# Four buffers for converted weight halves in a one-core attention-and-MLP kernel, with six relay buffers placed behind the mixing and the lead's score copies on ScalarE

## The chip, the cores and the metric

One core of a Trainium2 chip. The metric is the device time of one execution in microseconds (us). The engines are TensorE (PE, with its weight loads as PEld), VectorE (DVE), ScalarE (ACT), GpSimd (POOL) and SyncE (SP, which here only issues DMAs). The inputs are in HBM; wide scratch tensors in HBM (`x2`, `wsc`) are written and read back by the kernel itself.

## The reference, cut to what matters

```python
# q, k, v: (4, 12, 448, 64); w_pre, w_post: (12, 12); w_in: (768, 2048); w_out: (2048, 768); alpha: (2048,)
scores = np.matmul(q, k.transpose(0, 1, 3, 2)) / np.sqrt(64)
scores = np.einsum('bhij,hg->bgij', scores, w_pre)          # mix heads before the softmax
scores = scores - np.max(scores, axis=-1, keepdims=True)
attn = np.exp(scores)
attn = attn / (np.sum(attn, axis=-1, keepdims=True) + 1e-09)
attn = np.einsum('bhij,hg->bgij', attn, w_post)             # mix heads after the softmax
x = np.matmul(attn, v).transpose(0, 2, 1, 3).reshape(4 * 448, 768)
h = x @ w_in
g = np.maximum(h, 0.0) + alpha * np.minimum(h, 0.0)
out = g @ w_out
```

The two weight matrices arrive as 64-bit floats, so the kernel gets their raw 64-bit words and rounds them to 32-bit floats itself.

## The kernel before

The program has two streams of work that are interleaved by hand in one order (`manual_schedule`: each engine and each DMA queue executes its instructions in the order in which the code writes them). The loop `step(n)` runs for n from -1 to 94; most of the order is set there.

**Attention.** The queries of a batch are cut into chunks of 60 (or 30) rows. `qk` makes a chunk's raw scores in three parts (p = 0, 1, 2), each copied from PSUM into a score tile `st` (two buffers, tag `s`). `relay` moves rows of `st` by DMA on SP's queue into a mixing layout: groups of 10 query rows by 12 heads in `sr` tiles, which come from a ring of `NSR` constant buffers. Step n mixes groups 2n and 2n+1: `mix(n)` multiplies two `sr` tiles by `wk` on PE and VectorE takes the row maximum (`nm`, line 207); `exp(n)` follows on ScalarE (line 214), `norm(n-1)` on VectorE (lines 221 to 225), `post(n-2)` on PE (line 238) with a copy into `at` on ScalarE (line 244). When a set of chunks is complete, `pv` multiplies by v (line 261) and its two halves are added by ScalarE and VectorE into `xe` (lines 267, 268), which goes to `x2`. There are 90 mixing steps. PSUM is four double banks `p`, handed out in the order in which they were freed.

**Conversion.** `convert` goes through 64 half units (16 feature blocks, w_in and w_out, two halves of 384 columns). For each, GpSimd's queue fetches the raw words `cr` (four buffers), and `round_f64` runs five VectorE steps (lines 60, 64, 65, 66, 67) with two GpSimd operations between (lines 61, 62). Line 64 is the first to write `ct`, line 67 the last; then SP's queue stores `ct` to `wsc` (line 299). `ce` and `ct` have two buffers each. The order of the five steps of neighbouring units is woven: (i,0), (i,1), (i-1,3), (i-1,4), (i,2). In the lead (steps up to 26) a step of the program holds seven of these VectorE steps, later eight until the 64 units are done.

**MLP ("moe").** After the lead the four token blocks go through both weight matrices. `load_w` brings the converted weights `wr` back on GpSimd's queue, `split_w` splits each into a rounded part (ScalarE, line 340) and a remainder (GpSimd, line 341), and PE multiplies (lines 394 and 427). `split_x` does the same for the tokens on VectorE (lines 449, 450). `PACE` says how much of this work stands in each step.

**SP's queue.** At the start of `step(n)`, ahead of `mix(n)`, `relays(2 * (n + RA + 1))` orders the relays of two groups, which step n+3 will mix. A relay into an `sr` buffer waits until the mixing that read the buffer last is over. At the end of a step, `flush()` orders what was put into `later`: the stores of `ct`, of `xe` and of the output.

Of the kernel before, what the change touches and what calls it, by code (L numbers as in the profile page):

```python
# [8 lines left out]
F32 = mybir.dt.float32  # L9
F32R = mybir.dt.float32r  # L10
I32 = mybir.dt.int32
# [8 lines left out]
B, H, S, D = 4, 12, 448, 64  # L20
DM, DFF = 768, 2048
NT = B * S
HI = 5
HP = HI * H
# [8 lines left out]
NJ = S // 64  # L33
SR0 = 4
RA = 3
NSR = 2 * (RA + 1)
WARM = 12
LAG = 2
TB = [(b * S, S) for b in range(B)]
# [6 lines left out]
CU = DM // 2  # L46
# [24 lines left out]
def talking_heads_prelu(ctx: ExitStack, tc: tile.TileContext, q, k, v, w_pre, w_post, mask, w_in, w_out, alpha, out):  # L71
    nc = tc.nc
# [49 lines left out]
    alpha_sb = cst.tile([128, NFC], F32, name="alpha_sb")  # L122
    wk = cst.tile([128, 64], F32, name="wk")
    wq = cst.tile([128, H, HI], F32, name="wq")
    mask_sb = cst.tile([128, 2, HI, H], F32, name="mask_sb")
    wb = cst.tile([128, 2, H], F32, name="wb")
    sr_b = [cst.tile([128, S], F32, name=f"sr{i}") for i in range(NSR)]
    q_b = [cst.tile([128, 8 + NP * CW], F32, name=f"q{i}") for i in range(3)]
    a_t = cst.tile([128, NS, H, AW], F32, name="at")
# [5 lines left out]
    later = []  # L135
# [34 lines left out]
    def qk(ci, p, copy=nc.scalar.copy):  # L170
        b, c = chunks[ci]
        pt = grab()
        cn = CHUNKS[c][1]
        for cc in range(2):
            for r in range(2):
                h = slice(64 * r, 64 * r + 64)
                nc.tensor.matmul(pt[64 * cc:64 * cc + 64, r, :S], q_t[ci][h, (3 * cc + p) * cn + SR0 * cc:(3 * cc + p) * cn + SR0 * cc + 64],  # L177
                                 k_t[b, p][h, cc, :], start=True, stop=True)
        if p == 0:
            s_t[ci] = sp.tile([128, 2, 3, S], F32, tag="s", name=f"st{ci}")  # L180
        copy(s_t[ci][:, :, p, :], pt[:, :, :S])  # L181
        free(pt)
        done_qk.add((ci, p))
# [16 lines left out]
    def mix(n):  # L200
        to = m_t[n] = grab()
        ga, gb = sr_t.pop(2 * n), sr_t.pop(2 * n + 1)
        for hf, g in ((0, ga), (64, gb)):
            for u, r in ((0, slice(0, 64)), (1, slice(64, SR0 + GP))):
                nc.tensor.matmul(to[hf:hf + 64, u, :S], wk[r, :], g[r, :], start=True, stop=True)  # L205
        nm = sm.tile([128, 2], F32, tag="nm", name=f"nm{n}")
        nc.vector.tensor_reduce(out=nm, in_=to[:, :, :S], axis=AX.X, op=ALU.max, negate=True)  # L207
        nm_t[n] = nm
# [64 lines left out]
            in_=xe[:, :3 * cn].rearrange("p (c i) -> p c i", c=3)[:, :, skip:]))  # L273


    def flush():
        now, later[:] = list(later), []
        for f in now:
            f()

    def convert():
        todo = [(f, x, c) for f in range(NFC) for x in range(2) for c in range(0, DM, CU)]
        raw_c = {}

        def fetch_c(i):
            if i < len(todo):
                f, x, c = todo[i]
                raw_c[i] = cvp.tile([128, CU], I64, tag="cr", bufs=4, name=f"cr{f}_{x}_{c}")
                nc.gpsimd.dma_start(out=raw_c[i], in_=(w_in, w_out)[x][f, :, c:c + CU])

        def unit(i):
            f, x, c = todo[i]
            raw = raw_c.pop(i)
            e = cvp.tile([128, CU], I32, tag="ce", name=f"ce{f}_{x}_{c}")
            t = cvp.tile([128, CU], I32, tag="ct", name=f"ct{f}_{x}_{c}")
            for j, op in enumerate(round_f64(nc, raw, e, t)):
                op()
                if j == 4:
                    later.append(lambda: (stored.add((f, x, c)), nc.sync.dma_start(out=wsc[f, :, x * DM + c:x * DM + c + CU], in_=t.bitcast(F32))))
                    fetch_c(i + 4)  # L300
                yield

        for i in range(4):
            fetch_c(i)
        yield
        n = len(todo)
        seq = []
        for i in range(n + 1):
            seq += [(i, 0), (i, 1)] if i < n else []
            seq += [(i - 1, 3), (i - 1, 4)] if i else []  # L310
            seq += [(i, 2)] if i < n else []
        units = {}
        for i, j in seq:
            if j == 0:
                units[i] = unit(i)
            next(units[i], None)
            yield
# [156 lines left out]
    with tc.manual_schedule():  # L474
# [8 lines left out]
        nc.vector.memset(warm.bitcast(F32), 0.0)  # L483
        for _ in range(WARM):
            nc.tensor.matmul(pairs[3][:, 0, :S], warm[:, :128], warm, start=True, stop=True)
        nc.gpsimd.memset(mask_sb, 0.0)
        nc.gpsimd.memset(wb, 0.0)
        own = mask[:HP, :HI, :].rearrange("(i h) j g -> i h j g", h=H)
        wide = lambda w, n: w.rearrange("(o h) g -> o h g", o=1).to_broadcast([HI, n, H])
        for u in range(2):  # L490
# [30 lines left out]
        def relays(upto, dmas):  # L521
            nonlocal relayed
            while relayed < min(upto, NG) and (groups[relayed][0], NP // 2 - 1) in done_qk:
                relay(relayed, dmas)
                relayed += 1

        relays(4, (nc.sync, nc.scalar))
        relays(2 * (RA + 1), (nc.sync,))
        next(conv)
        for ci in (2, 3):  # L530
            load_q(ci)
# [28 lines left out]
        def step(n):  # L560
            step_now[0] = n
            if n == 1:
                for hx in range(2):
                    load_v(0, hx)
            if n >= 0:
                relays(2 * (n + RA + 1), (nc.sync,))
            due = pv_at.get(n)
            lead = n <= ready[0]
            pace = 0.0 if lead else PACE[min(cur, 2)]
            if live(n):  # L570
                mix(n)
            if live(n - 1):
                norm(n - 1)
            if due is not None:
                b = pvs[due][0]
                for hx in range(2):
                    pv(due, hx)
                    if due + 1 < len(pvs) and pvs[due + 1][0] != b:
                        load_v(b + 1, hx)
            if live(n - LAG):  # L580
                post(n - LAG)
            if live(n):
                exp(n)
            for ci, p in qk_at.get(n, []):
                b = chunks[ci][0]
                qk(ci, p, nc.vector.tensor_copy if lead and p == 1 else nc.scalar.copy)
                if ci + 1 < NC and chunks[ci + 1][0] != b:
                    load_k(b + 1, p)
                if p == 2 and ci + 3 < NC:
                    load_q(ci + 3)  # L590
            if lead:
                converts(CONV_LEAD)
            else:
                moe_work(n, pace * 0.5)
                converts(CONV_T0 // 2)
                moe_work(n, pace * 0.5)
                converts(CONV_T0 // 2)
            flush()
            for t in range(len(TB)):
                if n == ready[t] - 1:  # L600
                    load_x(t, 0)
                    load_x(t, 1)
                if n == ready[t] and t == 0:
                    for _ in split_x(0):
                        pass
                    nxt_x[0] = iter(())
            if n == ready[0] - 3:
                for u in range(2):
                    for x in range(2):
                        load_w(u, x)  # L610
                for u in range(2):
                    split_w(u, 0)
                    load_w(u + 2, 0)
# [43 lines left out]
```

## Time and profile before

| | us |
|---|---|
| median of 3 runs | 1092.49 (1086.48 to 1092.76) |
| the profiled execution's own time | 1092.34 |
| its span, first to last instruction | 1090.5 |
| PE busy | 894.5 (82%) |
| VectorE busy | 604.7 (55%) |
| ScalarE busy | 421.5 (39%) |
| GpSimd busy | 480.0 (44%) |

The busy shares are averages over stages that have different limits, so they don't say what bounds any of them. The profiled execution's own time is 1.84 us more than its span and within 0.2 us of the median, so a sum made against the profile can be carried to the median unchanged.

### The profile page before, as it was taken

Reading aid. Unit: us, or ns where it says so; the run is one execution under the profiler, and the core shown is the slowest. Engines: PE = TensorE matmul, PEld = TensorE weight load, DVE = VectorE, ACT = ScalarE, POOL = GpSimd, SP = SyncE. Lnnn points to the kernel's source line nnn. Section 1 sums busy time; section 2 is a strip of 40 time slices with the busy share of each in tenths; the row PEclk is TensorE's granted clock in tenths of the full one; section 3 lists DMA queues with packets and bytes.
Section 4 is the critical chain, followed back from the end, with each engine's and each line's share of the span. In section 5 each row is a group of like instructions: output and inputs, shape, how many; then the busy total and the mean of one; then the engine's idle time right before and its main releaser. Section 6 shows DMA issues by size and latency. Waiting matters only on the chain.

```text
span 1090.5 us, 28930 instructions
## 1 busy us (share of the span) xinstructions
PE 894.5 (82%) x12204; PEld 701.7 (64%) x12204; DVE 604.7 (55%) x1090; ACT 421.5 (39%) x769; POOL 480.0 (44%) x563
## 2 busy tenths in 40 slices
PE   5555564555777977879799999997999999899997
PEld 2234352345455656657578787786787888779996
DVE  4565664556596685774456444544645464354443
ACT  1333332322243433345445555643545454222220
POOL 6432333334364465543424553443235343447661
PEclk7767686685798988999999999999999999899999
DMA  7655566567466476544654454445544342444322
GB/s 184 201 157 175 161 168 158 163 175 229 133 187 191 142 196 189 168 136 126 184 171 131 135 157 125 134 124 161 178 123 138 120 119 73 121 124 126 102 78 76
DMA packets 79730, 161.82 MB, mean 148 GB/s; under 512 B 26276, under 2 KB 64304, under 8 KB 79600
## 3 DMA queue, kind: packets, MB, share of 16 engines
q0 software_dynamic: 21312, 90.58, 31.2%
q1 hardware_dynamic: 57432, 68.18, 18.7%
q8 instruction: 96, 1.57, 0.6%
q10 hardware_dynamic: 856, 1.21, 0.5%
q14 instruction: 34, 0.28, 0.1%
HBM read 97.62 MB, written 23.59 MB: 111 GB/s over the span
## 4 chain that ended last, share of the span: by engine, by line
PE 53%; DMA 22%; DVE 14%; issue 4%; POOL 2%; SPq 2%; ACT 1%; ACTq 0%; POOLq 0%; DVEq 0%
PE p L427 18%; PE p L394 17%; DMA wsc<-ct 17%; PE p L261 5%; PE p L238 5%; PE p L205 4%; PE p L177 4%; DVE ce L66 3%; DVE ct L67 3%; DMA sr<-st 2%; DVE ct L64 2%; POOL ws L341 2%; DVE nm L207 2%; SPq L198 1%; DMA xr<-x 1%
## 5 line engine op out<-in xcount | busy, mean ns | idle before, releaser
L341 POOL TENSOR_TENSOR ws<-wr,ws 128x768 fp32r<-128x768 f32 x128 | 235.9, 1843 | 277.9 <-ACT ws L340 276.2
L427 PE MATMUL p<-g,ws 128*128 128x448 f32 x1152 | 259.6, 380 | 23.5 <-POOL ws L341 13.1
L394 PE MATMUL p<-xs,ws 128*128 128x448 f32 x1152 | 258.9, 379 | 10.2 <-DVE xs L449 8.0
L427 PEld LDWEIGHTS p<-g,ws 128*128 128x128 f32 x1152 | 222.0, 195 | 63.0 <-POOL ws L341 17.0
L394 PEld LDWEIGHTS p<-xs,ws 128*128 128x128 f32 x1152 | 218.1, 193 | 53.9 <-issue 18.6
L214 ACT ACTIVATE e<-p,nm 128x448 f32<-128x448 f32 x180 | 112.5, 632 | 195.7 <-DVE nm L207 133.6
L238 PEld LDWEIGHTS p<-r,e 64*64 64x64 f32 x5040 | 113.7, 149 | 113.0 <-issue 68.9
L238 PE MATMUL p<-r,e 64*64 64x60 f32 x5040 | 119.5, 239 | 71.8 <-DVE r L225 34.0
L244 ACT COPY at<-p 128x960 f32<-128x960 f32 x88 | 86.3, 981 | 177.7 <-PE p L238 176.8
L340 ACT CAST ws<-wr 128x768 fp32r<-128x768 f32 x128 | 103.9, 844 | 117.8 <-issue 51.9
L207 DVE TENSOR_REDUCE nm<-p 128x2 f32<-128x896 f32 x90 | 97.7, 1086 | 90.2 <-PE p L205 90.0
L363 DVE TENSOR_TENSOR acc<-p,acc 128x896 f32<-128x896 f32 x84 | 91.3, 1087 | 87.5 <-PE p L427 87.4
L177 PE MATMUL p<-k,q 64*64 64x448 f32 x768 | 115.7, 655 | 23.0 <-DVE xe L268 8.4
L205 PE MATMUL p<-sr,wk 64*64 64x448 f32 (+1 forms) x720 | 102.5, 608 | 38.0 <-ACT at L249 12.4
L261 PEld LDWEIGHTS p<-at,v 64*64 64x64 f32 x3360 | 97.2, 150 | 34.6 <-ACT e L214 19.6
L261 PE MATMUL p<-at,v 64*64 64x120 f32 (+2 forms) x3360 | 99.5, 268 | 23.0 <-ACT e L214 17.1
L64 DVE TENSOR_SCALAR ct<-cr 128x384 int32<-128x384 int32 x64 | 29.7, 464 | 132.7 <-DMA wsc<-ct 132.7
L348 DVE TENSOR_SCALAR t<-p,alpha_sb 128x448 f32<-128x448 f32 x64 | 43.4, 678 | 93.9 <-PE p L394 93.9
L332 POOL DMA_DIRECT2D wr<-wsc x128 | 71.8, 561 | 39.4 <-POOL ws L341 34.7
L181 ACT COPY st<-p 128x896 f32<-128x896 f32 x84 | 74.9, 911 | 12.9 <-PE p L177 6.5
L205 PEld LDWEIGHTS p<-sr,wk 64*64 64x64 f32 (+1 forms) x720 | 28.6, 147 | 75.1 <-issue 40.5
L61 POOL TENSOR_SCALAR ce<-ce 128x384 int32<-128x384 int32 x64 | 33.4, 521 | 78.0 <-DVE ce L60 76.4
(48 smaller groups left out, 655.3 us busy)
## 6 DMA issues: line engine op xcount, KB each, us to landing
wr<-wsc POOLq DMA_DIRECT2D x128, 384.0 KB, 3.7
sr<-st SPq DMA_DIRECT2D x332, 105.0 KB
cr<-in_w_in_dram POOLq DMA_DIRECT2D x32, 384.0 KB, 4.0
cr<-in_w_out_dram POOLq DMA_DIRECT2D x32, 384.0 KB, 4.0
wsc<-ct SPq DMA_DIRECT2D x64, 192.0 KB
xr<-x SPq DMA_DIRECT2D x24, 224.0 KB
out_dram<-acc SPq DMA_DIRECT2D x12, 448.0 KB
q<-in_q_dram POOLq DMA_DIRECT2D x54, 90.0 KB, 4.3
```

The costliest lines, as they stand in the source:

```text
L177: nc.tensor.matmul(pt[64 * cc:64 * cc + 64, r, :S], q_t[ci][h, (3 * cc + p) * cn + SR0 * cc:(3 * cc + p) * cn + SR0 * cc + 64], k_t[b, p][ ...
L205: nc.tensor.matmul(to[hf:hf + 64, u, :S], wk[r, :], g[r, :], start=True, stop=True)
L207: nc.vector.tensor_reduce(out=nm, in_=to[:, :, :S], axis=AX.X, op=ALU.max, negate=True)
L214: nc.scalar.activation(out=e_t[n][:, u], in_=m_t[n][:, u, :S], func=AF.Exp, bias=nm_t[n][:, u:u + 1], scale=1.0, accum_out=se_t[n][:, u:u ...
L238: nc.tensor.matmul(dst[:, :, HI * u:HI * u + HI], e[h, u, 64 * jb:64 * jb + 64], r[h, u].rearrange("p (h i) -> p h i", h=H), start=True, s ...
L244: nc.scalar.copy(at[:, :, col:col + 2 * GI].rearrange("p q (g i) -> p g q i", g=2), pt[:, :, :NS * GP].rearrange("p g (q i) -> p g q i", i ...
L261: nc.tensor.matmul(to[64 * t:64 * t + 64, r, cl * cn:(cl + 1) * cn], v_t[b, hx][pr, s, (2 * cl + t) * D:(2 * cl + t + 1) * D], a_t[pr, s, ...
L340: nc.scalar.copy(t[:, 0], w)
L341: nc.gpsimd.tensor_tensor(t[:, 1], w, t[:, 0], ALU.subtract)
L363: nc.vector.tensor_tensor(dst, pt[:, :, :N], dst, ALU.add)
L394: nc.tensor.matmul(pt[:, f % 2, :S], w[:, tw, c * 128:(c + 1) * 128], xs[:, tx, c, :], start=(j == 0), stop=(j == 3 * NCC - 1))
L427: nc.tensor.matmul(pt[:, d, :S], w[:, tw, (c + d) * 128:(c + d + 1) * 128], g[:, tg], start=(j == 0), stop=(j == 3 * FG - 1))
```

## The change

Four edits. The `ct` tiles of the conversion get four buffers in place of two, and their stores go into a list `ripe` with the number of the step, which is emptied at the start of the next step (or at once when more than two wait, or when `load_w` asks). The relays of a step stand behind `mix(n)` in place of ahead of it, and the `sr` ring has six buffers in place of eight. In the lead the copies of the scores for p = 1, which VectorE made, go to ScalarE like the others. The constants `mask_sb` and `wb` lose tiles of their own and live in a buffer of the `xr` tag, which is first needed much later.

```diff
-NSR = 2 * (RA + 1)
+NSR = 2 * RA
...
-    mask_sb = cst.tile([128, 2, HI, H], F32, name="mask_sb")
-    wb = cst.tile([128, 2, H], F32, name="wb")
+    setup = xrp.tile([128, S], F32, tag="xr", name="setup")
+    mask_sb = setup[:, :2 * HP].rearrange("p (u j g) -> p u j g", u=2, g=H)
+    wb = setup[:, 2 * HP:2 * HP + 2 * H].rearrange("p (u g) -> p u g", u=2)
...
-    def flush():
+    ripe = []
+
+    def flush(upto=None):
+        while ripe and (upto is None or ripe[0][0] <= upto or len(ripe) > 2):
+            ripe.pop(0)[1]()
         now, later[:] = list(later), []
...
-            t = cvp.tile([128, CU], I32, tag="ct", name=f"ct{f}_{x}_{c}")
+            t = cvp.tile([128, CU], I32, tag="ct", bufs=4, name=f"ct{f}_{x}_{c}")
...
-                    later.append(lambda: (stored.add((f, x, c)), nc.sync.dma_start(out=wsc[f, :, x * DM + c:x * DM + c + CU], in_=t.bitcast(F32))))
+                    ripe.append((step_now[0], lambda: (stored.add((f, x, c)), nc.sync.dma_start(
+                        out=wsc[f, :, x * DM + c:x * DM + c + CU], in_=t.bitcast(F32)))))
...
-        relays(2 * (RA + 1), (nc.sync,))
+        relays(2 * RA, (nc.sync,))
...
-            if n >= 0:
-                relays(2 * (n + RA + 1), (nc.sync,))
             due = pv_at.get(n)
             lead = n <= ready[0]
             pace = 0.0 if lead else PACE[min(cur, 2)]
+            flush(n - 1)
             if live(n):
                 mix(n)
+            if n >= 0:
+                relays(2 * (n + RA + 1), (nc.sync,))
...
-                qk(ci, p, nc.vector.tensor_copy if lead and p == 1 else nc.scalar.copy)
+                qk(ci, p)
...
-            flush()
+            flush(n - 1)
```

**SP's queue in the lead.** The number behind a tile's name is that of its allocation; `wsc<-ct` is a store, `sr<-st` a relay of one group (two DMAs). Before, from the store of the fourth half unit on:

```order
L299 DMA wsc<-ct_1_384_298 128x384
L299 DMA wsc<-ct_0_0_343 128x384
L195 DMA sr_122<-st_283 60x1x448 x2
L195 DMA sr_123<-st_283 60x1x448 x2
L299 DMA wsc<-ct_0_384_418 128x384
L195 DMA sr_124<-st_283 60x1x448 x2
L195 DMA sr_125<-st_283 60x1x448 x2
L299 DMA wsc<-ct_1_0_485 128x384
```

The same place now:

```order
L304 DMA wsc<-ct_1_384_292 128x384
L304 DMA wsc<-ct_0_0_337 128x384
L196 DMA sr_117<-st_277 60x1x448 x2
L196 DMA sr_118<-st_277 60x1x448 x2
L304 DMA wsc<-ct_0_384_412 128x384
L196 DMA sr_119<-st_277 60x1x448 x2
L196 DMA sr_120<-st_277 60x1x448 x2
L304 DMA wsc<-ct_1_0_479 128x384
```

The sequence of stores and relays is the same, because nothing else stands on SP's queue between the end of one step and the start of the next; what changed is the ring behind the `sr` names (six numbers in place of eight), so that a relay of step n fills the buffers that `mix(n)` has just read, where it filled those of `mix(n-1)`.

**SP's queue at the end of the lead**, where the tokens `xr` of the first block are loaded from `x2`. Before:

```order
L271 DMA x_57<-xe_0_2643 128x3x28
L271 DMA x_57<-xe_1_2688 128x3x28
L299 DMA wsc<-ct_0_384_2566 128x384
L439 DMA xr_2_2752<-x_57 128x448
L439 DMA xr_3_2756<-x_57 128x448
L439 DMA xr_4_2760<-x_57 128x448
L439 DMA xr_5_2764<-x_57 128x448
L195 DMA sr_122<-st_2396 60x1x448 x2
```

Now:

```order
L272 DMA x_57<-xe_0_2637 128x3x28
L272 DMA x_57<-xe_1_2682 128x3x28
L445 DMA xr_2_2745<-x_57 128x448
L445 DMA xr_3_2749<-x_57 128x448
L445 DMA xr_4_2753<-x_57 128x448
L445 DMA xr_5_2757<-x_57 128x448
L304 DMA wsc<-ct_0_384_2560 128x384
L196 DMA sr_117<-st_2390 60x1x448 x2
```

One store has moved behind four token loads; one step earlier another has moved behind two. These are the only two places of the whole program at which SP's sequence of stores, relays and loads differs.

**VectorE in a step of the lead.** `nm`, `s` and `r` are the row maximum and the normalization, `ct` and `ce` the conversion. Before:

```order
L207 TENSOR_REDUCE nm_651<-p_132 128x2
L221 TENSOR_SCALAR s_653<-se_617 128x2
L222 RECIPROCAL s_653<-s_653 128x2
L225 TENSOR_TENSOR r_656<-wq,s_653 128x120
L181 COPY st_695<-p_131 128x2x448
L64 TENSOR_SCALAR ct_1_0_640<-cr_1_0_557 128x384
L66 SCALAR_TENSOR_TENSOR ce_0_384_628<-cr_0_384_492,ce_0_384_628 128x384
```

Now:

```order
L208 TENSOR_REDUCE nm_641<-p_129 128x2
L222 TENSOR_SCALAR s_647<-se_611 128x2
L223 RECIPROCAL s_647<-s_647 128x2
L226 TENSOR_TENSOR r_650<-wq,s_647 128x120
L64 TENSOR_SCALAR ct_1_0_634<-cr_1_0_551 128x384
L66 SCALAR_TENSOR_TENSOR ce_0_384_622<-cr_0_384_486,ce_0_384_622 128x384
```

The score copy is gone from VectorE here, and at ten more places; apart from these eleven and two memsets for the missing `sr` buffers, VectorE's order is the same. The eleven copies stand on ScalarE now, between the exponentials of a step and the copy `at` of the next.

## Rows read from the trace of the kernel before

**Rows 1.** The chain that ended last: shares of the span by engine, then by line

```profile
PE 53%; DMA 22%; DVE 14%; issue 4%; POOL 2%; SPq 2%; ACT 1%; ACTq 0%; POOLq 0%; DVEq 0%
PE p L427 18%; PE p L394 17%; DMA wsc<-ct 17%; PE p L261 5%; PE p L238 5%; PE p L205 4%; PE p L177 4%; DVE ce L66 3%; DVE ct L67 3%; DMA sr<-st 2%; DVE ct L64 2%; POOL ws L341 2%; DVE nm L207 2%; SPq L198 1%; DMA xr<-x 1%
```

**Rows 2.** Stretches: length, busy by engine (instructions), PE clock, DMA share, GB/s

```profile
26.80:263.10 236.30, 130.42 (x2636) 88.89 (x2628) 137.86 (x305) 78.99 (x161) 86.20 (x150) 0.73 0.60 176
263.10:291.80 28.70, 18.95 (x320) 13.76 (x320) 10.71 (x26) 4.45 (x9) 4.45 (x8) 0.64 0.59 171
291.80:474.10 182.30, 144.45 (x1786) 108.70 (x1786) 136.58 (x235) 70.69 (x128) 101.92 (x129) 0.90 0.59 170
508.50:936.00 427.50, 411.77 (x6254) 330.42 (x6246) 215.58 (x368) 209.19 (x383) 182.92 (x170) 0.99 0.47 136
```

**Rows 3.** VectorE's waits, 26.8 to 263.1 us: total us, times, longest

```profile
DVE ct L64 <- DMA wsc<-ct: 92.4, 35, 8.6
DVE nm L207 <- PE p L205: 5.2, 1, 5.2
```

**Rows 4.** VectorE's waits, 291.8 to 474.1 us

```profile
DVE ct L64 <- DMA wsc<-ct: 34.7, 16, 6.4
DVE t L348 <- PE p L394: 6.7, 2, 3.4
```

**Rows 5.** Timeline, 101 to 108 us, VectorE and SP's queue: start, length, idle before

```profile
101.49 0.56 DVE L67 TENSOR_TENSOR ct<-ct,ce 128x384 f32<-128x384 f32 x1
...
101.97 0.55 DVE L65 SCALAR_TENSOR_TENSOR ct<-cr,ct 128x384 f32<-128x384 uint32 x1
102.08 0.33 SPq L299 DMA_DIRECT2D wsc<-ct  x1
...
102.51 3.39 SPq L195 DMA_DIRECT2D sr<-st  x4
...
106.10 0.36 DVE L64 TENSOR_SCALAR ct<-cr 128x384 int32<-128x384 int32 x1 [3.31 <-DMA wsc<-ct]
106.38 1.08 DVE L207 TENSOR_REDUCE nm<-p 128x2 f32<-128x896 f32 x1
```

**Rows 6.** Groups by line and shape, 26.8 to 263.1 us: busy us, mean ns

```profile
L207 DVE TENSOR_REDUCE nm<-p 128x2 f32<-128x896 f32 x27 | 29.3, 1084 | 5.2 <-PE p L205 5.2
...
L62 POOL TENSOR_SCALAR ce<-ce 128x384 int32<-128x384 int32 x36 | 18.9, 525 | 3.0
L61 POOL TENSOR_SCALAR ce<-ce 128x384 int32<-128x384 int32 x36 | 18.1, 503 | 47.1 <-DVE ce L60 46.7
L181 ACT COPY st<-p 128x896 f32<-128x896 f32 x20 | 18.1, 904 | 3.6 <-PE p L177 1.4 <-PE p L205 1.1 <-DMA sr<-st 1.1
...
L181 DVE COPY st<-p 128x896 f32<-128x896 f32 x11 | 12.0, 1092 | 2.5 <-DMA sr<-st 1.8 <-PE p L177 0.3
```

**Rows 7.** DMA issues, 26.8 to 263.1 us: KB each, us to landing

```profile
cr<-in_w_in_dram POOLq DMA_DIRECT2D x18, 384.0 KB, 4.0
...
v<-in_v_dram POOLq DMA_DIRECT2D x4, 576.0 KB, 9.1
```

**Rows 8.** Waits of the whole span, ScalarE for weights that come back

```profile
ACT ws L340 <- DMA wr<-wsc: 12.0, 2, 10.2
```

**Rows 9.** Timeline, 250 to 259 us: one pv on PE, and a collision of VectorE and GpSimd

```profile
250.93 1.82 POOL L341 TENSOR_TENSOR ws<-wr,ws 128x768 fp32r<-128x768 f32 x1
250.98 2.19 DVE L65 SCALAR_TENSOR_TENSOR ct<-cr,ct 128x384 f32<-128x384 uint32 x1
...
253.38 5.16 PE L261 MATMUL p<-at,v 64*64 64x30 f32 x165
```

**Rows 10.** A stretch in which the DMA engines were full (columns as in rows 2)

```profile
160.00:170.00 10.00, 7.46 (x274) 6.57 (x268) 4.35 (x11) 4.02 (x9) 5.04 (x9) 0.78 1.01 242
```

**Rows 11.** Waits of the whole span, TensorE for relayed rows

```profile
PE p L205 <- DMA sr<-st: 7.1, 2, 6.1
```

**Rows 12.** Waits of SP's queue over the whole span, for the mixing

```profile
SPq L195 <- PE p L205: 79.6, 39, 7.0
```

More of the change, by code (lines that the diff above doesn't have):

```diff
@@ L485, in talking_heads_prelu @@
             nc.tensor.matmul(pairs[3][:, 0, :S], warm[:, :128], warm, start=True, stop=True)
-        nc.gpsimd.memset(mask_sb, 0.0)
-        nc.gpsimd.memset(wb, 0.0)
+        nc.gpsimd.memset(setup[:, :2 * HP + 2 * H], 0.0)
         own = mask[:HP, :HI, :].rearrange("(i h) j g -> i h j g", h=H)
```

## The prediction

> **What bounds the kernel now.** I first read the chain that ended last [rows 1]. TensorE has half of it, most of that in the last 580 us: from 508.5 to 936 us it is busy 411.8 of 427.5 us at a clock of 0.99 [rows 2], and nothing in this change takes work from it. The entry to look at is the 17% of the DMA `wsc<-ct`. A store can only be on the chain if somebody waits for it to land. So I cut the span at the starts of the row maxima of steps 0, 26, 27 and 44 and read each stretch for itself [rows 2]: A, 26.8 to 263.1 us (26 steps of the lead); B, 263.1 to 291.8 (the step in which the first tokens are loaded and split); C, 291.8 to 474.1 (the MLP has begun, the conversion still runs).
>
> In A no engine is full: TensorE 130.4, VectorE 137.9, ScalarE 79.0, GpSimd 86.2 of 236.3 us, and the clock is 0.73, a mixture of the two levels 1.2 and 2.4 GHz. The waits say which engine sets the pace. VectorE waited 92.4 us in 35 pieces for stores of `ct`, and once for 5.2 us for the mixing [rows 3]; 137.9 + 92.4 + 5.2 = 235.5 of 236.3 us, so it is always at work or waiting for a store. The timeline shows one round [rows 5]: line 67 finishes a `ct` at 102.05, SP issues its store at 102.08, and line 64, which wants that buffer, starts at 106.10, after an idle 3.31 us. The row maximum of the next step stands behind line 64 on VectorE, so it starts at 106.38, and the whole attention step hangs on it. A step takes 9.1 us on average (the 27 row maxima [rows 6] begin 26 steps in 236.3 us). In C the same wait takes 34.7 us in 16 pieces [rows 4], with TensorE at 144.5 and VectorE at 136.6 of 182.3 us.
>
> **The change part by part.**
>
> *Four `ct` buffers.* With two, line 64 of unit k+2 needs the store of unit k. In the woven order only two VectorE operations lie between line 67 of k and line 64 of k+2 (line 65 of k+1, line 60 of k+2), some 1 us (0.55 us for line 65 [rows 5], the other is shorter) against the 4.05 us that the store takes in rows 5. With four, line 64 of unit k+4 needs it, and ten more operations lie between, twelve in all. A step holds seven, so this is 12/7 of a step. VectorE's own work is 137.9 - 12.0 (the moved copies, below) = 125.9 us in 26 steps, 4.8 us each, so at its fastest the distance is 12/7 x 4.8 = 8.3 us. The store must wait for SP at worst through one set of relays, 3.39 us [rows 5], and then 4 us: 7.4 us. So an ordinary store comes back in time, and the 92.4 us go. A store of the slow kind (8.6 us [rows 3]) comes back after 12.0 and costs some 3.7 us.
>
> *What is late next in A.* VectorE's work and its other waits, 125.9 + (236.3 - 137.9 - 92.4 = 6.0) = 131.9 us. TensorE's 130.4 us and the DMA engines' 0.60 x 236.3 = 141.8 us [rows 2] come close beside it, and they hardly met before because all of them waited together. I add what appears when the steps close up. Five `pv` lie in A, and VectorE's adds to `xe` stand behind them; one half of such a `pv` pair took TensorE half of 5.16 us [rows 9], which nothing covers if TensorE is no longer ahead: 5 x 2.6 = 13 us. ScalarE stood still 12.0 us for the first weights that come back [rows 8], its exponentials behind it; half of it reaches VectorE: 6 us. Three stretches of about 10 us have full DMA engines (one is rows 10); there the store above and the fetch of `cr` (4.0 us, but 9.1 us for the large loads it shares a queue with [rows 7], against a distance of eleven operations, 7.5 us) come late, 3 us each: 9 us. Together 131.9 + 13 + 6 + 9 = 160 us. The DMA engines would then be busy 141.8/160 = 0.89 of the time and TensorE 0.82, at today's clock; denser work may raise that clock, which I don't count. A gains 236.3 - 160 = 76 us. Its bounds: 142 us, the DMA engines' own time (gain 94), and the rivals below.
>
> *B.* Its chain is load of v, `pv`, store to `x2`, token loads, split; stores of `ct` have one small part in it. Now two of them stand behind token loads on SP, and behind them the relays as before. Nobody needs these stores soon, four buffers cover them. Gain between 0 and 5 us; I take 2.
>
> *C.* VectorE's work with its other waits is 182.3 - 34.7 = 147.6 us; TensorE's 144.5 us of work at the 96% that it reaches from 508.5 us on are 150.5. With two engines so near each other, and TensorE waiting for VectorE in places, I don't expect 150.5: I take 162, a little more than half of the way. Gain 20; bounds 0 and 32.
>
> *Relays behind the mixing, six buffers.* Relays of step n now wait for `mix(n)`, where they waited for `mix(n-1)`, and SP's queue waits with them: the next stores of `ct` and `xe`, token loads and output stores stand behind. A store of step n is made by VectorE after the row maximum of step n, which itself waits for `mix(n)`; so SP is held from nothing that could go earlier, but for the 3.39 us of issuing. The relays are needed by `mix(n+3)`. At 160/26 = 6.2 us a step these are 18 us, less 3.39 for issue and up to 9.1 (the slowest landing that rows 7 show) leaves 5 us. Later, at about 10 us a step, it is 15 and more. TensorE waited for relays 7.1 us in the whole span, in two pieces [rows 11], though SP's queue already waited for the mixing 39 times [rows 12]. I take nothing; bounds 0 and +6.
>
> *Eleven copies from VectorE to ScalarE.* Minus 11 x 1.09 = 12.0 us on VectorE, plus 11 x 0.90 = 9.9 us on ScalarE [rows 6], which has 79.0 of 160 us and carries 88.9 then. It is in the sum above. A new wait is possible: the copies wait for relays that still read the score buffer, and exponentials stand behind them. VectorE met this once, 1.8 us [rows 6].
>
> *The shared setup tile* is over long before its buffer is needed, and two memsets less run at a time when VectorE has nothing else: 0.
>
> **The sum.** 76 + 2 + 20 = 98 us off the profiled 1092.3 us: **994 us**, the same against the median. With each part at its best bound, 94 + 5 + 32 = 131: 961.
>
> **The rivals.**
>
> *The DMA engines bind.* In A they moved 176 GB/s x 236.3 us = 41.6 MB; when full they moved 242 GB/s [rows 10], which makes 172 us. If the 13 and 6 us of `pv` and weights don't overlap with this, A takes 191 us and gains 45; C, with later arrivals, gains 10; B 2. That is 57: **1035 us**. For it: three stretches are full today. Against it: over all of A the share is 0.60, so most bytes move without crowding. The Trainium skill ("DMA: Bandwidth & Descriptors", section Specifications) puts the limit from HBM at about 358 GB/s for one core; by that the 41.6 MB would be 116 us, an estimate from that page, and this rival would fall. No stretch of 10 us here that I show reaches it, so the measured rate stands.
>
> *VectorE and GpSimd get in each other's way more.* At 250.9 us a GpSimd subtraction and line 65 started together, and line 65 took 2.19 us [rows 9] where it takes 0.55 alone [rows 5]. Lines 61 and 62 occupy GpSimd 18.1 + 18.9 = 37 us in A [rows 6]. With VectorE idle for 92 us these had room; packed, each may hold up a VectorE operation. Half of them on top of A gives 178.5, a gain of 58; C, in which GpSimd is busy 101.9 us, gains 10; B 2: 70 in all, **1022 us**; all of them on top of A, 1041. This is a rule of the Trainium skill as well ("SBUF — State Buffer", section Who interferes with whom): a VectorE instruction with two SBUF inputs and a GpSimd instruction that reads SBUF share a port, and the second to start stands still for all of the first. The trace agrees, 2.19 against 0.55 us.
>
> *It doesn't do what it says.* The wait for the store is replaced by another of the same length on the same chain, the fetch of `cr` or SP's queue: **about 1088 us**, the copies' part left over. Against it: the distance of 8.3 us worked out above, and no wait for `cr` in rows 3.
>
> *Slower.* The relays land after `mix(n+3)` wants them, since they can't start before `mix(n)`, and TensorE waits for them from step 27 to 89, where its time is the kernel's. To be slower it has to lose more than 98 us in 63 steps, 1.6 us a step; at 1.8 us, 113 us: **1107 us**. It decides from a time of three steps, some 30 us there, between `mix(n)` and the landing. Rows 5 and 7 show 3.4 + 9.1 = 12.5.
>
> **How the numbers follow.** Chances: the forecast, between 961 and 1012 us, 0.62; DMA engines 0.13; VectorE with GpSimd 0.14; better than all bounds (a higher clock in A) 0.04; nothing moves 0.04; slower 0.03. A measurement of this kernel can tell about 1%, 11 us, from no change: the first four cases are faster, 0.93; 0.04 the same; 0.03 slower. The range from 958 to 1040 takes in the first three cases up to their ends.
>
> **What the next profile would show.** Right: VectorE's wait at line 64 for `wsc<-ct` falls from 92.4 us in A and 34.7 in C to under 25 together; the steps of the lead take about 6.2 us; step 27 begins near 214 us in place of 292; VectorE is over 70% busy in A and the DMA share over 0.8; the last 580 us keep their length. Wrong by a rival: the DMA share in A at 1.0 with stores of over 8 us; or lines 65 to 67 with means well over 0.6 us; or TensorE waiting at line 205 for `sr<-st`. The prediction falls if the steps of the lead stay at 9 us although line 64 no longer waits: then another engine's chain had the same length all along. A smaller miss would come from C, if TensorE's waits there are not VectorE's doing.

## The result, and the profile after

The changed kernel takes 1002.91 us (median of 4 runs, 998.6 to 1005.61) against 1090.8 us before (median of four runs; the 1092.49 ahead of the prediction is that of three of them): a ratio of 0.920, 95% interval 0.915 to 0.924. 994 was forecast, with 958 to 1040 as the range. The profiled execution has a span of 1002.6 us.

The chain that ended last, by engine and by line (the changed file's lines are one to six higher than before: 208 is the row maximum that was 207, 304 the store that was 299, 347 the subtraction on GpSimd that was 341):

```profile
PE 61%; DVE 13%; DMA 10%; issue 7%; POOL 4%; ACT 3%; SPq 1%; POOLq 0%; ACTq 0%; DVEq 0%
PE p L433 20%; PE p L400 19%; PE p L262 7%; DMA sr<-st 6%; PE p L239 6%; PE p L206 5%; PE p L178 4%; POOL ws L347 2%; DVE nm L208 2%; DVE ce L66 2%; DMA wsc<-ct 2%; DVE g L361 1%; DMA xr<-x 1%; DVE ct L65 1%; DVE ct L64 1%
```

The stores `wsc<-ct` had 17% of the chain [rows 1] and have 2%. The relays have taken a part of their place, 6% in place of 2.

The same stretches as in [rows 2], cut at the same row maxima (A, B, C, and the rest): length, then busy us of PE, PEld, VectorE, ScalarE and GpSimd with instructions, clock, DMA share, GB/s:

```profile
25.90:195.80 169.90, 119.28 (x2636) 76.52 (x2628) 129.17 (x294) 86.23 (x171) 93.02 (x150) 0.80 0.84 246
195.80:222.10 26.30, 17.82 (x320) 12.46 (x320) 11.20 (x26) 4.58 (x11) 4.92 (x9) 0.69 0.60 183
222.10:380.90 158.80, 137.90 (x1785) 103.85 (x1785) 142.53 (x235) 70.82 (x128) 103.82 (x129) 0.93 0.68 196
380.90:1002.60 621.70, 589.95 (x7410) 485.79 (x7408) 310.21 (x498) 263.15 (x467) 270.75 (x242) 0.98 0.44 128
```

A fell from 236.3 to 169.9 us, B from 28.7 to 26.3, C from 182.3 to 158.8; the rest, which was 1090.5 - 474.1 = 616.4, grew to 621.7, and the start is 0.9 us shorter. Together that is 66.4 + 2.4 + 23.5 - 5.3 + 0.9 = 87.9 us, the difference of the two spans. (The prediction calls the end of C step 44. Counted, it is the row maximum of step 42, and this is how I cut here. The times of the stretch are not touched by it.)

VectorE's waits in A, after [rows 3]:

```profile
DVE nm L208 <- PE p L206: 19.0, 6, 5.7
DVE nm L208 <- ACT st L182: 8.5, 1, 8.5
DVE xe L269 <- ACT xe L268: 7.7, 6, 1.9
DVE ct L64 <- DMA wsc<-ct: 5.5, 2, 4.5
DVE xe L269 <- DMA sr<-st: 2.3, 1, 2.3
```

One of the six pieces of the first line, 5.58 us, ends where A begins and so lies ahead of it; the other five are 13.4 us. The same holds for the 5.2 us of [rows 3], which the prediction counts into A. The first row maximum after, and before (start, length, idle before):

```profile
25.94 1.09 DVE L208 TENSOR_REDUCE nm<-p 128x2 f32<-128x896 f32 x1 [5.58 <-PE p L206]
26.77 1.09 DVE L207 TENSOR_REDUCE nm<-p 128x2 f32<-128x896 f32 x1 [5.19 <-PE p L205]
```

Of the 26 steps in A, 17 take 4.3 to 5.4 us, nearly all of it VectorE's work; the other nine take 6.4 to 13.3 us and hold 84.6 of the 169.9 us. The timeline of one of the short ones, which answers to [rows 5] (start, length):

```profile
82.94 0.74 DVE L67 TENSOR_TENSOR ct<-ct,ce 128x384 f32<-128x384 f32 x1
83.60 1.08 DVE L208 TENSOR_REDUCE nm<-p 128x2 f32<-128x896 f32 x1
83.70 0.33 SPq L304 DMA_DIRECT2D wsc<-ct  x1
84.12 3.38 SPq L196 DMA_DIRECT2D sr<-st  x4
...
85.93 0.36 DVE L64 TENSOR_SCALAR ct<-cr 128x384 int32<-128x384 int32 x1
...
88.50 1.08 DVE L208 TENSOR_REDUCE nm<-p 128x2 f32<-128x896 f32 x1
```

Line 67 ends at 83.68 and line 64 starts at 85.93 without any idle time ahead of it, 2.2 us after the store was issued, a way that takes 4 us in [rows 5]; the next row maximum begins 4.9 us after the last one. That is the 4.8 us of pure VectorE work on which the prediction's distance was worked out. The wait at line 64 is 5.5 us in the whole span, where it was 132.7:

```profile
L64 DVE TENSOR_SCALAR ct<-cr 128x384 int32<-128x384 int32 x64 | 29.7, 464 | 132.7 <-DMA wsc<-ct 132.7
```

### The profile page after: what moved, and what is told of

The parts are those of the page before. It is cut to its first block, busy times and chain, and to the rows that moved or that the text cites. A ratio compares the mean times of both kernels' runs of the same rounds, so it can differ in the third digit from the quotient of the medians.

```text
span 1002.6 us, 28904 instructions
## 1 busy us (share of the span) xinstructions
PE 877.3 (87%) x12204; PEld 685.0 (68%) x12204; DVE 602.6 (60%) x1077; ACT 428.8 (43%) x780; POOL 489.3 (49%) x562
## 3 DMA queue, kind: packets, MB, share of 16 engines
q0 software_dynamic: 21312, 90.58, 33.6%
## 4 chain that ended last, share of the span: by engine, by line
PE 61%; DVE 13%; DMA 10%; issue 7%; POOL 4%; ACT 3%; SPq 1%; POOLq 0%; ACTq 0%; DVEq 0%
PE p L433 20%; PE p L400 19%; PE p L262 7%; DMA sr<-st 6%; PE p L239 6%; PE p L206 5%; PE p L178 4%; POOL ws L347 2%; DVE nm L208 2%; DVE ce L66 2%; DMA wsc<-ct 2%; DVE g L361 1%; DMA xr<-x 1%; DVE ct L65 1%; DVE ct L64 1%
## 5 line engine op out<-in xcount | busy, mean ns | idle before, releaser
L400 PEld LDWEIGHTS p<-xs,ws 128*128 128x128 f32 x1152 | 216.3, 191 | 51.7 <-issue 13.4
L239 PEld LDWEIGHTS p<-r,e 64*64 64x64 f32 x5040 | 107.5, 141 | 67.4 <-issue 43.4
L239 PE MATMUL p<-r,e 64*64 64x60 f32 x5040 | 112.4, 229 | 27.7 <-issue 12.0
L178 PE MATMUL p<-k,q 64*64 64x448 f32 x768 | 107.7, 611 | 24.4 <-ACT st L182 13.1
L206 PE MATMUL p<-sr,wk 64*64 64x448 f32 (+1 forms) x720 | 106.6, 614 | 25.6 <-ACT at L250 9.3
L262 PEld LDWEIGHTS p<-at,v 64*64 64x64 f32 x3360 | 90.7, 143 | 18.9 <-issue 16.5
L262 PE MATMUL p<-at,v 64*64 64x120 f32 (+2 forms) x3360 | 91.7, 257 | 7.1 <-issue 3.6
L182 ACT COPY st<-p 128x896 f32<-128x896 f32 x95 | 84.2, 913 | 30.4 <-DMA sr<-st 20.1
L161 POOL DMA_DIRECT2D q<-in_q_dram x62 | 38.3, 626 | 79.7 <-PE p L178 79.6
L61 POOL TENSOR_SCALAR ce<-ce 128x384 int32<-128x384 int32 x64 | 36.7, 574 | 67.9 <-DVE ce L60 65.4
```

Of the source, the lines that this page charges most:

```text
L239: nc.tensor.matmul(dst[:, :, HI * u:HI * u + HI], e[h, u, 64 * jb:64 * jb + 64], r[h, u].rearrange("p (h i) -> p h i", h=H), start=True, s ...
L262: nc.tensor.matmul(to[64 * t:64 * t + 64, r, cl * cn:(cl + 1) * cn], v_t[b, hx][pr, s, (2 * cl + t) * D:(2 * cl + t + 1) * D], a_t[pr, s, ...
L400: nc.tensor.matmul(pt[:, f % 2, :S], w[:, tw, c * 128:(c + 1) * 128], xs[:, tx, c, :], start=(j == 0), stop=(j == 3 * NCC - 1))
```

## The experiments

Each experiment changes the changed kernel by a few lines, but for the ninth, which starts from the kernel before. In one view, the medians, and the lengths of A, B and C, of steps 42 to 89, and of what follows, read from the row maxima of one profiled execution each, which need not be at its kernel's median:

| kernel | median us | A | B | C | 42 to 89 | rest |
|---|---|---|---|---|---|---|
| before | 1090.8 | 236.3 | 28.7 | 182.3 | 434.8 | 181.6 |
| changed | 1002.9 | 169.8 | 26.3 | 158.8 | 439.1 | 182.6 |
| two `ct` | 1091.1 | 234.4 | 29.8 | 180.4 | 437.5 | 182.1 |
| three `ct` | 1006.4 | 175.9 | 23.4 | 159.3 | 437.6 | 181.8 |
| copies on VectorE | 1010.8 | 176.5 | 25.3 | 158.8 | 439.5 | 182.5 |
| stores as before | 1003.4 | 168.7 | 24.5 | 159.6 | 439.1 | 182.3 |
| no fetches | 984.5 | 158.1 | 22.0 | 154.0 | 441.2 | 181.9 |
| no lines 61, 62 | 988.7 | 170.5 | 25.2 | 150.0 | 438.1 | 181.3 |
| later split | 999.0 | 163.3 | 28.8 | 158.0 | 438.6 | 181.9 |
| three `ct`, eight `sr` | 1004.4 | 175.0 | 24.1 | 158.0 | 435.9 | 180.9 |
| before with three `ct` | 1009.8 | 181.1 | 23.3 | 158.6 | 437.9 | 181.6 |
| later split, lead of 8 | 996.7 | 171.1 | 24.7 | 152.1 | 441.1 | 182.2 |
| later split, lead of 6 | 1002.9 | 155.2 | 26.3 | 173.4 | 438.3 | 181.9 |

**Two `ct` buffers again, the rest of the change kept** (the stores go back to the end of the step with it).

```diff
-            t = cvp.tile([128, CU], I32, tag="ct", bufs=4, name=f"ct{f}_{x}_{c}")
+            t = cvp.tile([128, CU], I32, tag="ct", name=f"ct{f}_{x}_{c}")
...
-                    ripe.append((step_now[0], lambda: (stored.add((f, x, c)), nc.sync.dma_start(
-                        out=wsc[f, :, x * DM + c:x * DM + c + CU], in_=t.bitcast(F32)))))
+                    later.append(lambda: (stored.add((f, x, c)), nc.sync.dma_start(out=wsc[f, :, x * DM + c:x * DM + c + CU], in_=t.bitcast(F32))))
```

> The changed kernel with two ct buffers again (and the stores ordered at the end of the step, which two buffers need); the relays behind the mixing, the six sr buffers and the copies on ScalarE stay. Main theory (the two further ct buffers carry nearly all of the gain): 1075 to 1092 us, VectorE's wait at line 64 for stores back over 100 us. Rival (the copies or the relay order carry a good part): 1010 to 1060 us.

It takes 1091.14 us, ratio 1.001 (0.998 to 1.004) to the kernel before: without the buffers nothing of the gain is left. Its waits of the whole span and stretch A:

```profile
DVE ct L64 <- DMA wsc<-ct: 144.9, 54, 6.9
```

```profile
26.60:261.00 234.40, 134.00 (x2636) 87.50 (x2628) 123.27 (x293) 87.48 (x172) 86.02 (x150) 0.73 0.60 177
```

VectorE has 14.6 us less work in A than before (137.86 in [rows 2]), 12.0 of them the copies, and A is only 1.9 us shorter: the wait in the whole span grew from 132.7 to 144.9 us. As long as the stores set the pace, work taken from VectorE turns into waiting. (The copies, the relays' order and the smaller ring are all in this run; it shows that together they are worth nothing here, not what each is worth.)

**Three `ct` buffers.**

```diff
-            t = cvp.tile([128, CU], I32, tag="ct", bufs=4, name=f"ct{f}_{x}_{c}")
+            t = cvp.tile([128, CU], I32, tag="ct", bufs=3, name=f"ct{f}_{x}_{c}")
```

> The changed kernel with three ct buffers in place of four. Between line 67 of unit k and line 64 of unit k+3 lie seven operations, one step, 4.8 us at the least, against 4 us for a store and up to 7.4 us when SP is at its relays. Main theory (the distance must cover SP's relays and the landing): a part of the wait comes back, 15 to 50 us at line 64, and the time is 1010 to 1035 us. Rival (one buffer more than two is all that was needed): 1000 to 1006 us.

1006.36 us (1003.39 to 1010.36). The main theory's 1010 to 1035 was too high: most of what four buffers give, three give as well; its runs and those with four buffers (998.6 to 1005.61) overlap. But a part of the wait is there again, in the amount that was expected:

```profile
DVE ct L64 <- DMA wsc<-ct: 26.3, 13, 8.0
```

13 waits against 2 with four buffers, and A is 6 us longer in the profile. That A lost only 6 us for 20.8 us more of waiting suggests that other chains of the lead are close behind.

**The copies for p = 1 on VectorE again.**

```diff
-                qk(ci, p)
+                qk(ci, p, nc.vector.tensor_copy if lead and p == 1 else nc.scalar.copy)
```

> The changed kernel with the lead's copies for p = 1 on VectorE again (11 x 1.09 us). If VectorE is the strict pace of the lead: 1010 to 1016 us. If DMA engines, relays and VectorE share the pace: 1001 to 1009. If the copies hurt on ScalarE, where they wait for relays with the exponentials behind them (11.4 us of such waits in the lead now): 993 to 1000.

1010.81 us (1009.45 to 1017.48), at the lower edge of what a strict pace by VectorE would give; A is 6.7 us longer for 11.6 us more of VectorE's work. So the copies are worth some 8 us here.

**The stores in the list of the end of the step, four buffers.**

```diff
-                    ripe.append((step_now[0], lambda: (stored.add((f, x, c)), nc.sync.dma_start(
-                        out=wsc[f, :, x * DM + c:x * DM + c + CU], in_=t.bitcast(F32)))))
+                    later.append(lambda: (stored.add((f, x, c)), nc.sync.dma_start(out=wsc[f, :, x * DM + c:x * DM + c + CU], in_=t.bitcast(F32))))
```

> The changed kernel with the stores of ct in the list of the end of the step again; four buffers stay. SP's sequence differs at two stores around the token loads only. Main theory: no change, 999 to 1007 us. Rival (the two stores behind the token loads cost or save a wait in the step of the split): 985 to 997 or 1009 to 1020 us.

1003.37 us: no change. Ordering the stores a step later moved two of them on SP's queue and cost or gave nothing.

**Without the fetches of raw words.**

```diff
+                if i >= 4:
+                    raw_c[i] = raw_0[i % 4]
+                    return
-                raw_c[i] = cvp.tile([128, CU], I64, tag="cr", bufs=4, name=f"cr{f}_{x}_{c}")
+                raw_c[i] = raw_0[i] = cvp.tile([128, CU], I64, tag="cr", bufs=4, name=f"cr{f}_{x}_{c}")
```

> The changed kernel without the fetches of raw words after the first four: later half units convert these four tiles again, so the weights are wrong. In the lead this takes away 36 x 384 KB of the 41.8 MB, more of the DMA engines' time, and 36 issues of 0.6 us on GpSimd. If the DMA engines (share 0.84) hold up the lead: its 26 steps fall from 170 to under 155 us and the time to 970 to 987 us. If VectorE's own work and TensorE hold it: 993 to 1001.

984.51 us, in the range that speaks for the DMA engines, but A's own 158.1 us misses the 155 that I had set: A gives 11.7 us, and B and C another 4.3 and 4.8, so the total alone doesn't decide about the lead. Stretch A of this run:

```profile
25.30:183.40 158.10, 109.83 (x2636) 72.12 (x2628) 129.15 (x293) 86.44 (x171) 71.87 (x114) 0.85 0.57 179
```

The DMA share falls from 0.84 to 0.57 with VectorE's work the same, 129.15 us, and A gets 11.7 us shorter. With this much room on the DMA engines VectorE is busy 0.82 of the stretch. GpSimd loses its issues too, and TensorE's clock in A is 0.85 in place of 0.80, with 9.5 us less of its work, so the 11.7 us are an upper bound for the crowding by the fetches alone. Where they come from can be read: in A VectorE no longer waits for a store (5.5 us in the changed kernel), and it waits 8.0 us for the mixing where it waited 13.4.

**Without lines 61 and 62 on GpSimd.**

```diff
-    yield lambda: (g_clamp(), g_scale(),
-                   v.tensor_scalar(out=t, ...
+    yield lambda: (
+                   v.tensor_scalar(out=t, ...
```

> The changed kernel without the two GpSimd operations of a half unit (lines 61 and 62), so the converted exponents are wrong. In the lead lines 65, 66 and 67 take 582, 689 and 643 ns on average where 551, 552 and 558 are their medians before, some 9 us in all. If the collisions with GpSimd cost VectorE this and the lead hangs on it: 988 to 997 us, with means near 555 ns. Rival (they are hidden behind DMA and TensorE): 999 to 1006 us, although the means fall.

988.72 us (987.66 to 993.51). The median lies where the first theory put it, but the profile shows the gain in another place. Lines 65 to 67 in A, first of the changed kernel, then of this run (count, busy us, mean ns, idle before):

```profile
L66 DVE SCALAR_TENSOR_TENSOR ce<-cr,ce 128x384 int32<-128x384 int32 x36 | 24.8, 689 | 0.4 <-POOL ce L62 0.4
L67 DVE TENSOR_TENSOR ct<-ct,ce 128x384 f32<-128x384 f32 x36 | 23.2, 643 | 1.1
L65 DVE SCALAR_TENSOR_TENSOR ct<-cr,ct 128x384 f32<-128x384 uint32 x37 | 21.5, 582 | 0.0
```

```profile
L65 DVE SCALAR_TENSOR_TENSOR ct<-cr,ct 128x384 f32<-128x384 uint32 x37 | 20.4, 550 | 0.0
L67 DVE TENSOR_TENSOR ct<-ct,ce 128x384 f32<-128x384 f32 x36 | 20.0, 557 | 1.1
L66 DVE SCALAR_TENSOR_TENSOR ce<-cr,ce 128x384 int32<-128x384 int32 x36 | 19.9, 554 | 0.0
```

and the stretches A and C of this run:

```profile
26.60:197.20 170.60, 115.37 (x2636) 75.54 (x2628) 118.47 (x294) 85.52 (x171) 47.98 (x78) 0.83 0.82 243
222.30:372.30 150.00, 138.45 (x1792) 105.57 (x1792) 129.66 (x235) 71.19 (x128) 74.28 (x81) 0.93 0.71 206
```

The collisions are real: the means go back to 550 to 557 ns, and VectorE's work in A falls by 10.7 us. A is as long as it was, 170.6 against 169.9. In C, where VectorE was busy 142.5 of 158.8 us, its work falls by 12.9 and the stretch by 8.8. So in this profile the collisions of the lead lie under something else, and those of C are on the chain. Two things limit that reading. The profiled execution took 993.51 us, the longest of the four by 4 us, and its span is 10.9 us shorter than the changed kernel's where the medians differ by 14.2; where the faster executions save the rest, in A or elsewhere, no profile shows. And GpSimd's own work goes with the collisions: in C the chain that ended last has 7.2 us on GpSimd in the changed kernel and none here, so the 8.8 us may be in part GpSimd's.

**The first two splits of w_in two steps after their loads.**

```diff
+            if n == ready[0] - 1:
+                for u in range(2):
+                    split_w(u, 0)
+                    load_w(u + 2, 0)
             if n == ready[0] - 3:
                 for u in range(2):
                     for x in range(2):
                         load_w(u, x)
-                for u in range(2):
-                    split_w(u, 0)
-                    load_w(u + 2, 0)
```

> The changed kernel with the first two weight splits of w_in ordered two steps after their loads in place of right behind them. ScalarE no longer waits for the loads (7.7 us now, with TensorE 9.3 and VectorE 8.5 us behind it in the lead). If this wait is on the lead's chain: 993 to 999 us. If something else ends as late: 1000 to 1006 us.

998.98 us (995.85 to 999.89), at the upper edge of the first case; the runs overlap with those of the changed kernel (998.6 to 1005.61). What it removes stands in the timeline of the changed kernel (start, length, idle before):

```profile
174.98 2.18 POOL L338 DMA_DIRECT2D wr<-wsc  x4
...
180.87 0.83 ACT L346 CAST ws<-wr 128x768 fp32r<-128x768 f32 x1 [6.07 <-DMA wr<-wsc]
...
185.18 1.77 PE L206 MATMUL p<-sr,wk 64*64 64x448 f32 x8 [9.35 <-ACT at L250]
...
187.17 1.09 DVE L208 TENSOR_REDUCE nm<-p 128x2 f32<-128x896 f32 x1 [8.48 <-ACT st L182]
```

ScalarE stood at the split until its weights had landed, TensorE waited for ScalarE's copy, and VectorE for the mixing behind it. With the later split that step takes 4.9 us in place of 13.3; A is 6.5 us shorter, B 2.5 us longer.

**Three `ct` and eight `sr` buffers** (four and eight have no room), so that a relay waits for the mixing of the step before, as it used to.

```diff
-NSR = 2 * RA
+NSR = 2 * (RA + 1)
...
-            t = cvp.tile([128, CU], I32, tag="ct", bufs=4, name=f"ct{f}_{x}_{c}")
+            t = cvp.tile([128, CU], I32, tag="ct", bufs=3, name=f"ct{f}_{x}_{c}")
```

> The kernel with three ct buffers and eight sr buffers (there is no room for four and eight); the relays stay behind the mixing in the program but wait for the mixing of the step before, as in the kernel before the change. To be held against the run with three ct buffers and six sr buffers (1006.4 us). Main theory (six buffers cost nothing): 1003 to 1010 us. Rival (SP's wait for the mixing of the same step delays relays and stores in the lead): 992 to 1002 us.

1004.37 us (1002.06 to 1006.51), against 1006.36 with six: the two can't be told apart. A is 175.0 against 175.9 us. With three `ct` buffers the smaller ring is free, or nearly.

**The kernel before with three `ct` buffers and nothing else** (the shared setup tile makes the room).

```diff
-            t = cvp.tile([128, CU], I32, tag="ct", name=f"ct{f}_{x}_{c}")
+            t = cvp.tile([128, CU], I32, tag="ct", bufs=3, name=f"ct{f}_{x}_{c}")
```

> The kernel before with three ct buffers (room for them from the shared setup tile, no more) and no other edit: eight sr buffers, relays ahead of the mixing, stores at the end of the step, copies for p = 1 on VectorE. Main theory (the buffers carry the gain, the copies some 8 us on top once VectorE no longer waits, the rest nothing): 1008 to 1018 us. Rival (relay order or ScalarE's copies are needed for the gain): over 1025 us.

1009.82 us (1007.0 to 1011.07), ratio 0.926 (0.923 to 0.929), with 15.4 us of waits at line 64. One buffer of 1.5 KB per partition brings 81 of the 88 us. Against the changed kernel with three buffers (1006.36) the other edits together are worth 3.5 us, with runs that overlap.

**Eight and six conversion steps in a step of the lead**, both with the later split.

```diff
-CONV_LEAD, CONV_T0 = 7, 8
+CONV_LEAD, CONV_T0 = 8, 8
```

> The later splits (999 us) with eight conversion steps in a step of the lead in place of seven. 27 VectorE operations move from the stage after the lead, where collisions with GpSimd make them 0.5 to 0.8 us long and VectorE is 90% busy, into the lead, where it is 79% busy. If VectorE sets the pace of the later stage and not of the lead: 988 to 996 us. If both hang on it alike: 997 to 1003. If the lead is the tighter of the two: over 1003 us.

996.72 us (993.54 to 999.24), between the first two cases: the lowest of the kernels that do the whole work, but inside the noise of the 999 with seven.

> The later splits (999 us) with six conversion steps in a step of the lead in place of seven, the opposite of the run with eight. If the lead is the tighter stage: 990 to 996 us. If VectorE sets the pace of the stage after it: 1002 to 1012 us. If both alike: 997 to 1002.

1002.86 us (1000.65 to 1004.16), at the foot of what VectorE's pace in the later stage would give. The table shows the trade: from six to seven to eight, A takes 155.2, 163.3 and 171.1 us, C 173.4, 158.0 and 152.1, with 155.1, 143.1 and 126.0 us of VectorE's work in C. Eight further microseconds of lead each time buy 15 the first time and 6 the second. Seven and eight lie near the bottom.

## Why the prediction held, point by point

*The wait for the store goes.* Shown. It was right in its cause (two buffers alone bring the whole loss back, and one buffer more in the kernel before brings 81 of the 88 us), in its place (A and C), and in its size: 132.7 us of waiting fell to 5.5, under the 25 that were set. The distance worked out for four buffers, 8.3 us at the least, was enough. It was generous: three buffers, whose distance is seven operations, one step of 4.8 us, leave 26.3 us of waits and still give nearly all of the time. One row was misread on the way: 8.6 us is the longest wait at line 64, not the time of a store; that store was issued at 163.09 and line 64 started at 173.98, 10.9 us later.

*What is late next in A: 160 us.* Measured: 169.9, so the gain there was 66.4 and not 76. The term most mis-sized is the crowding of the DMA engines, for which I took 9 us in three stretches. In the sum the waits for the mixing and for late DMAs were 6.0 + 9 = 15 us; measured are 13.4 for the mixing, 5.5 for stores and 3.3 in small pieces, 22.2. At 0.84 the share is high nearly everywhere in A, and the run without fetches, which has a share of 0.57, takes 158.1, 11.7 us less (an upper bound, as said). Its waits for the mixing and for stores are 10.9 us shorter. By the chain that ended last it is above all the relays that come late, and for these the sum has no term. The chain has 42.5 us on them in A (start, length), where before it had 12.1 and without the fetches 12.6:

```profile
37.17 9.43 DMA sr<-st
60.23 3.19 DMA sr<-st
115.09 16.34 DMA sr<-st
144.40 5.51 DMA sr<-st
176.03 8.03 DMA sr<-st
```

With three `ct` buffers the chain has 33.6 us on relays and 32.9 on stores with six `sr`, 13.0 and 52.0 with eight, and A is as long; so neither of the two alone can be called the cause.

The longest of these pieces meets the six loads of k for the next batch, 224 KB each, ordered from 110.5 to 116.9 us (columns as in the stretches):

```profile
112.00:116.00 4.00, 3.26 (x72) 2.03 (x76) 3.97 (x8) 3.17 (x6) 3.32 (x6) 0.72 0.95 242
116.00:120.00 4.00, 2.46 (x92) 1.93 (x84) 3.90 (x11) 2.44 (x6) 3.79 (x7) 0.85 1.04 242
120.00:124.00 4.00, 3.18 (x109) 3.18 (x111) 2.15 (x6) 0.31 (x1) 1.86 (x4) 0.57 1.04 243
124.00:128.00 4.00, 0.56 (x29) 0.42 (x23) 1.55 (x4) 0.00 (x0) 1.01 (x2) 0.93 0.94 227
```

The DMA engines are full for 16 us, and from 124 on VectorE, TensorE and ScalarE nearly stand still: this one step takes 12.6 us. Without the fetches it still takes 10.5, so the fetches are 2 us of it; what the k loads are worth was not tried. The other terms were near, and in part they cancel: VectorE's work 129.2 against 125.9 (collisions, as the run without lines 61 and 62 shows), its waits for `xe` 10.0 (7.7 and 2.3) against 13, its wait behind the first weights 8.5 against 6. The later split takes 4 us off the median, with runs that overlap.

*The first rival, 1035 us, was too dark; the second, 1022, right in its mechanism and wrong in its place.* The DMA engines moved 246 GB/s on average over A, more than the 242 that I took for a full stretch, and still left VectorE 76% busy. The 242 were one stretch's rate and no ceiling: in the kernel before, from 33 to 43 us, engines with a share of 0.98 moved 284 GB/s. The estimate of 116 us that stands against this rival uses a limit for HBM, but about 11 of the 41.6 MB are relays from SBUF to SBUF. VectorE's collisions with GpSimd did grow (line 66 from 639 to 689 ns on average in A, line 67 from 562 to 643), but the profile shows no cost of them there, and at most 8.8 us in C. The Trainium skill's rule on the shared port ("SBUF — State Buffer", section Who interferes with whom) fits what is seen in A: take the GpSimd operations away and the means of VectorE's two-input operations, 582 to 689 ns, go down to 550 to 557.

*B: 2, C: 20.* Measured 2.4 and 23.5. C came to 158.8 us with VectorE at 142.5 and TensorE at 137.9 us of work. VectorE is the nearer limit there: from six to seven steps in the lead its work in C falls by 12.0 us and C by 15.4. From seven to eight 17.1 us less of work bring only 5.9, so something else is next.

*The relays behind the mixing: nothing; the copies: 12 us of VectorE's work.* For the ring the first is not contradicted: with three `ct` buffers, eight `sr` buffers in place of six move the time by 2 us, inside the noise. But the relays do come late, as the chain shows. ScalarE's waits for relays at the score copies did appear, 11.4 us in three pieces in A where they were 1.1, and 8.4 without the fetches; what they are worth was not tried by itself. The copies are worth about 8 us with four `ct` buffers. With two, the three edits other than the buffers are together worth nothing.

*The rest keeps its length.* It grew by 5.3 us, 4.3 of them in steps 42 to 89. Every variant lies between 435.9 and 441.2 there, one profile each, the kernel before at 434.8; eight `sr` buffers show 435.9, two `ct` with six `sr` 437.5, and the kernel before with three `ct`, which has the old ring and relay order, 437.9. So the ring is not needed for it; single profiles can't say more, and it stays open.

*The total.* 87.9 us against 98. A gave 9.6 us less than forecast and the rest 5.3 less, C gave 3.5 more, B and the start 1.3 more. That the median came within 9 us of the forecast owes a little to misses that cancel, but the path of the gain is the one that was worked out.

## What to carry to other kernels

When an in-order engine is idle only in front of one buffer, count the operations between the last write of that buffer and its next first write, multiply by the engine's own pace, and compare with the store's whole way (queue ahead of it, issue, landing): here 1 us stood against 4, one more buffer made it 4.8 us, and that alone brought 81 of 88 us. Ask the order of the edits as well: the copies were worth 8 us once the stores no longer set the pace, and while they did, copies, relay order and ring together were worth nothing. And after such a step look at each stage anew, since the next limit was not the same one in both: in the lead VectorE's work with what comes late from crowded DMA engines, behind it VectorE's work with its collisions.

## What the runs showed of the hardware that was not expected

Collisions that lengthen an engine's instructions by 10.7 us in a stretch need not show in its length: without the GpSimd operations VectorE's work in A fell from 129.2 to 118.5 us, and in the one profile of it A stayed at 170. The median landing of the fetches went only from 4.0 [rows 7] to 6.1 us while the traffic in A went from 176 to 246 GB/s:

```profile
cr<-in_w_in_dram POOLq DMA_DIRECT2D x18, 384.0 KB, 6.1
```

TensorE's clock in the same stretch rose from 0.73 to 0.80, with its work falling from 130.4 to 119.3 us for the same instructions.
